# Five zero matmuls in place of seven, the first piece of x copied out of PSUM in halves, both its value projections ahead of the second piece, and a fill of ones moved behind the fifth piece

## The chip, the core and the metric

The kernel runs on one core of a Trainium2 chip. The core has five engines with queues of their own: TensorE (PE; its weight loads are listed apart as PEld), VectorE (DVE), ScalarE (ACT), GpSimd (POOL) and SyncE (SP), which here only issues DMAs. An engine takes its instructions in the order in which they were written and waits on semaphores for the others. The metric is device time in microseconds, the median of the runs of one program. One execution was also profiled.

## The reference

Two branches of one input x (2048 rows of 640 numbers, bf16) are mixed by a gate. The first is a long convolution, done by a Fourier transform. The second is an attention with 32 heads of 20 numbers, in which each row looks at 8 rows, two apart. The start of the kernel works for the second branch.

```python
qkv = (x @ wqkv).reshape(B, S, 3, H, Dh).transpose(2, 0, 3, 1, 4)
q, k, v = qkv[0], qkv[1], qkv[2]
# each row looks at the rows s, s-2, ..., s-14
attn = softmax(mask(einsum("bhsd,bhswd->bhsw", q, kg) * scale))
b = einsum("bhsw,bhswd->bhsd", attn, vg).transpose(0, 2, 1, 3).reshape(B, S, D) @ wo
return g * a + (1 - g) * b
```

## The kernel before

x comes in eight pieces of 256 rows (`xn`, DMAs of 320 KB on SyncE's queue, line 413). For each piece TensorE makes ten transposes of 128 x 128 (line 445): five for its even rows, five for its odd rows, which lie apart because the attention looks two rows back. One copy (line 245 on VectorE, line 243 on ScalarE) brings the result from PSUM to `xT`. The value projection (`vproj`, line 521) takes 121 rows of `xT` and the first half of Wv, five matmuls of 320 columns a unit, and its result goes by a cast into `VW`. The query and key projections (`qkproj`, line 568) take five matmuls of 342 or 349 columns a unit, and their results go by a cast into `stg`, from where DMAs bring each head's rows to `qb` and `kb` (line 618) for the scores.

`VW` holds for each head 20 values and a 21st column of ones, so that the matmul of the attention weights gives the sum of the weights as well. The ones are written by a memset of 576 single elements in each partition, 42 bytes apart (line 431), and for 7 rows of two blocks the column is set to zero (line 433, 32 elements each). Both stand at the start of VectorE's queue, behind a memset of zeros (line 398), which the first matmuls read, and one of `ETall` (line 430).

Seven matmuls of zeros (line 401, `WARM`) keep TensorE busy until the first piece lands. Four more, of 512 columns, follow the transposes of the first piece (line 447); nobody reads what they write. They are called fills here.

What stands where isn't chosen by a scheduler. Each part of the work is a generator that asks for one step after the other, and a string of letters (`ORDER`) says whose step comes next; a dash takes the second of the engines that the step allows (in "AD", VectorE). `a` is the transposes and copies of x, `w` the first half of the value projection, `i` the query and key projection. PSUM is handed out in four slots by the same list. A piece is marked as ready for its readers (`xT0` to `xT7`) when its copy has been written down.

Of the kernel before, what the change touches and what calls it, by code (L numbers as in the profile page):

```python
# [18 lines left out]
D = 640  # L19
L = 4096  # L20
H = 32
DH = 20
NDT = 5
# [5 lines left out]
NBP = 9  # L29
NB = 2 * NBP  # L30
PRE = 7
X0 = 16
HS = 1024
HP = HS + 16
XW = X0 + 2 * HP
# [9 lines left out]
PL = 40  # L45
QC = 160
CR = 8
WARM = 7
KROWS = [(42, 64), (20, 42), (0, 20)]
TAIL = [(0, 3), (3, 3), (6, 2), (8, 3), (11, 3), (14, 2)]  # L50
LAND = dict(W0=9600.0, Wv0=5600.0, W1=23000.0, Wv1=25500.0, x=[4200.0, 7000.0, 8100.0, 10700.0, 11800.0, 12900.0, 14000.0, 15200.0], k=[20300.0])
# [61 lines left out]

STREAMS = "abcdefghijklmnopqrstuvwxyz0123456789ABCDEFGHIJKLMNOPQRSTUVWXYZ"
ORDER = """
a-aa-aw-wa-aw-ww-wiiai-iiaaiaa-aia-iii-aiaa-ii-iiii-ii-iiiicifffccccw-wwww-wwwwfwwwwf-wffffwwwwwwcwcccccwwwdw-wdwddddi-wfccccccii
-iiidfifddiiiieiifiiffiieidddiiiiiicddiwdxwexxxxxxxxxxccccffcfffffffffeccc-xcfcccccccccccccccccccccccccccccccccccccccccccidi-iiddd
ii-iddifd-iifxdddxedidffdfddefcicccii-iddiedd-icddlie-iiiyf-yddccdixiyyfy-xe-ydddexixdxddyyfyy-xcccxcccxffcccccccccccccciiiiciiccd
ciieddffdcccffdd-iiieiifiidididxdiffffffexididxdfeidid-i-xfxxyyy-yyexyey-xyyfyxccccccccciccccc-xcccc-idddidx-i-xxddddi-x-ijdddfjff
# [96 lines left out]
def kernel(  # L216
# [14 lines left out]
    nc = tc.nc  # L231
# [6 lines left out]
    def raw(ap, off, dims):  # L238
        return bass.AP(tensor=ap.tensor, offset=ap.offset + off, ap=dims)

    def copy(eng, dst, src):
        if eng == "A":
            nc.scalar.copy(dst, src)  # L243
        else:
            nc.vector.tensor_copy(dst, src)  # L245
# [7 lines left out]
    def psum(g, k=0, dt=F32):  # L253
        b = g.banks[k]
        v = PS[:, b[0], b[1]] if isinstance(b, tuple) else PS[:, b]
        return v.bitcast(dt) if dt != F32 else v
# [12 lines left out]
    VW = p0.tile([128, NB, H, DH + 1], BF, name="VW", tag="VW")  # L269
# [27 lines left out]
    xT = pL.tile([128, NDT, XW], BF, name="xT")  # L297
# [9 lines left out]
    def ev(name):  # L307
        if name not in E:
            E[name] = Ev()
        return E[name]  # L310

    def mark(name, g, lag=0.0):
        x = ev(name)
        x.src, x.lag = g.done.src, lag

    def at(name, t):
        ev(name).src, ev(name).lag = -1, t
# [73 lines left out]
    def masks(e):  # L391
        nc.gpsimd.memset(ksets[e][:, KW:], 0.0)
        nc.gpsimd.tensor_copy(ksets[e][:, 0:KW].rearrange("p (b k) -> p b k", k=BK), mm[:, 0:BK].unsqueeze(1).to_broadcast([128, NB, BK]))
        nc.gpsimd.tensor_copy(qsets[e][:].rearrange("p (b k) -> p b k", k=BQ), mm[:, BK:BK + BQ].unsqueeze(1).to_broadcast([128, NB, BQ]))

    def heads():
        z = pab[:, 0].rearrange("p n c -> p (n c)")
        nc.vector.memset(z, 0.0)
        wu = PS[:, 0]
        for n in range(WARM):  # L400
            nc.tensor.matmul(wu[:, n % 2, :], lhsT=z[:, 0:128], rhs=z[:, 0:512], start=True, stop=True, skip_group_check=True)
        nc.scalar.dma_start(ident[:], ca["ident"].ap())
        nc.scalar.dma_start(mm[:], ca["mm"].ap())
        at("ET", 4000.0)
        for a in range(8):
            if a == 1:
                nc.sync.dma_start(Wv[:, :, 0:320], W3[:, :, 2, 0:320])
                at("Wv0", LAND["Wv0"])
            if a == 3:
                for w in range(2):  # L410
                    nc.sync.dma_start(Wqk[:, :, w, 0:128], W3[:, :, w, 0:128])
                    at(f"W0{w}", LAND["W0"])
            nc.sync.dma_start(xn[:, a], raw(x2, 256 * a * D, [[2 * D, 128], [D, 2], [1, D]]))
            at(f"x{a}", LAND["x"][a])
        n0, n1 = KROWS[0]
        for q in range(4):
            nc.sync.dma_start(wraw[32 * q:32 * q + 32].rearrange("p c j -> p (c j)"), raw(A_shift_k, 4 * QC * q, [[0, 32], [1, 4 * QC]]))
        for q in range(4):
            nc.sync.dma_start(kin[32 * q:32 * q + 32, 3 + n0:3 + n1, :], raw(k2, n0 * D + QC * q, [[64 * D, 32], [D, n1 - n0], [1, QC]]))
        for q in range(4):  # L420
            at(f"k0{q}", LAND["k"][0])
        for w in range(2):
            nc.sync.dma_start(Wqk[:, :, w, 128:D], W3[:, :, w, 128:D])
            at(f"W1{w}", LAND["W1"])
        nc.sync.dma_start(Wv[:, :, 320:640], W3[:, :, 2, 320:640])
        at("Wv1", LAND["Wv1"])
        nc.gpsimd.memset(xT[:, :, 0:X0], 0.0)
        for c in range(2):
            nc.gpsimd.memset(xT[:, :, X0 + HP * c + HS:X0 + HP * (c + 1)], 0.0)
        nc.vector.memset(ETall[:, :, :, 3 * BQ:], 1.0)  # L430
        nc.vector.memset(VW[:, :, :, DH], 1.0)
        for j in (0, NBP):
            nc.vector.memset(VW[0:PRE, j, :, DH], 0.0)
        for q in range(4):
            nc.gpsimd.memset(kin[32 * q:32 * q + 1, 0:3, :], 0.0)
        for e in range(3):
            masks(e)

    def xpose():
        for a in range(8):  # L440
            g = yield Req("P", 0.0, [ev(f"x{a}")], take=1, pe=(10, 53.0, 110.0, 53.3) if a else (14, 98.8, 200.0, 98.8))
            tx = psum(g, dt=BF)
            for e in range(2):
                for dt in range(NDT):
                    nc.tensor.transpose(tx[:, e, 128 * dt:128 * dt + 128], xn[:, a, e, 128 * dt:128 * dt + 128], ident[:])
            for n in range(0 if a else 4):
                nc.tensor.matmul(PS[:, 3, 0], lhsT=ident[:], rhs=xn[:, 0, n % 2, 0:512], start=True, stop=True, skip_group_check=True)
            r = yield Req("AD", dict(A=1120.0, D=735.0), [g.done], give=g.banks)
            dst = xT[:, 0:1, X0 + 128 * a:X0 + 128 * a + 128]
            dst = raw(dst, 0, [dst.ap[0], [HP, 2], [XW, NDT], [1, 128]])  # L450
            copy(r.eng, dst, tx[:, :, 0:128 * NDT].rearrange("p e (t n) -> p e t n", t=NDT))
            mark(f"xT{a}", r)
        mark("xtr", g)

    def h0_slot():
# [437 lines left out]
    def final():  # L893
# [3 lines left out]
        for n, (t0, m) in enumerate(TAIL):  # L897
# [30 lines left out]
            for gg in range(4):  # L928
                (nc.scalar if n == len(TAIL) - 1 and gg > 1 else nc.sync).dma_start(raw(outf, (32 * (gg // 2) + gg % 2 + 2 * t0) * D, [[64 * D, 32], [2 * D, m], [1, D]]),
                                  reg[32 * gg:32 * gg + 32])  # L930

    heads()
    for gen in (xpose, h0_slot, fragger, score_gen, pv_gen, conv, conv_v, conv_end, qkproj, gate, x_slot, h_slot, p2_slot,
                u_slot, swaps, load_T, load_wo, op_tr, outproj, final):
        plan.add(gen(), gen.__name__)
# [34 lines left out]
```

## Time and profile before

| | |
|---|---|
| median of 3 runs | 224.88 us (224.69 to 225.51) |
| span of the profiled execution, first to last instruction | 222.5 us |
| what the median has above that span | 2.4 us |
| TensorE busy | 204.3 us, 92% of the span |
| VectorE busy | 185.0 us, 83% |
| ScalarE busy | 174.9 us, 79% |
| GpSimd busy | 51.1 us, 23% |

For the profiled execution no time of its own is listed beside its span. A row of the timeline gives start and length in microseconds, the engine, the line, the operation, what it writes and reads, the shape and the count; in brackets stands the idle time of the engine ahead of it, and what ended that. "issue" means that the engine waited for nothing that the profile shows. The chain of work that ended last is followed back from the last instruction to what released each step. DVE, ACT and POOL rows have measured lengths; matmuls are pipelined and their ends are modelled.

### The profile page before, as it was taken

The numbers are of one execution on the slowest core, as the hardware profiler recorded it, in microseconds if no ns is written. First come the engines' busy times: TensorE is split into PE (matmuls) and PEld (weight loads), VectorE is DVE, ScalarE is ACT, GpSimd is POOL, SyncE is SP. The second block draws the span as 40 slices with busy tenths as digits, with TensorE's granted clock in tenths as the row PEclk, the third lists the DMA queues.
The fourth block names the chain that finished last, engine by engine and source line by source line (L and its number), as shares of the span: only waits on it lengthen the run. The fifth ranks groups of instructions, "written<-read, shape, count | busy, mean of one in ns | idle before, by whom it ended". The sixth has DMA issues, their size and how long they took to land.

```text
span 222.5 us, 8401 instructions
## 1 busy us (share of the span) xinstructions
PE 204.3 (92%) x3577; PEld 165.8 (75%) x3577; DVE 185.0 (83%) x261; ACT 174.9 (79%) x253; POOL 51.1 (23%) x129
## 2 busy tenths in 40 slices
PE   7999999999999999699997867999999999979990
PEld 3777987696777577466685756889888899979880
DVE  4745778997998898569898978998999997859992
ACT  0264487769998898599999988998999999478770
POOL 7980711470617044402450000000000000000000
PEclk9999999999999999999999699999999999999999
DMA  6999789599999999803993396678567082003645
GB/s 199 349 237 275 188 180 205 133 168 149 208 182 197 163 151 155 140 4 52 183 171 74 85 214 152 172 174 213 122 142 227 4 184 55 3 3 91 152 106 136
DMA packets 69049, 33.35 MB, mean 150 GB/s; under 512 B 51476, under 2 KB 66708, under 8 KB 69012
## 3 DMA queue, kind: packets, MB, share of 16 engines
q1 hardware_dynamic: 65684, 27.66, 61.3%
q0 software_dynamic: 2880, 4.90, 9.9%
q8 instruction: 28, 0.46, 1.0%
q10 hardware_dynamic: 448, 0.26, 0.4%
q14 instruction: 9, 0.07, 0.1%
HBM read 19.51 MB, written 2.62 MB: 100 GB/s over the span
## 4 chain that ended last, share of the span: by engine, by line
PE 51%; DVE 20%; ACT 10%; DMA 8%; issue 7%; POOL 2%; DVEq 0%; POOLq 0%; ACTq 0%
PE PS L568 14%; PE PS L521 8%; ACT ETall L650 6%; PE PS L835 6%; DMA kb<-stg 6%; DVE UC L245 5%; PE PS L869 4%; PE PS L724 4%; PE PS L674 3%; DVE SX L245 3%; PE PS L642 3%; DVE q L926 2%; DVE yb L245 2%; ACT H L243 2%; DVE q L924 2%
## 5 line engine op out<-in xcount | busy, mean ns | idle before, releaser
L650 ACT ACTIVATE ETall<-PS 121x912 bf16<-121x912 f32 (+1 forms) x80 | 63.8, 864 | 8.1 <-PE PS L642 7.7
L568 PE MATMUL PS<-xT,Wqk 128*128 128x342 bf16 (+1 forms) x300 | 49.7, 310 | 0.6 <-ACT stg L243 0.3
L243 ACT CAST UC<-PS 128x1024 bf16<-128x1024 f32 (+2 forms) x49 | 44.4, 1030 | 4.0 <-DVE UC L245 3.1
L568 PEld LDWEIGHTS <-Wqk 128*128 128x128 bf16 x300 | 27.4, 97 | 14.3 <-issue 0.5
L521 PE MATMUL PS<-WvT,xT 128*121 128x320 bf16 x180 | 27.5, 300 | 0.1
L467 DVE TENSOR_TENSOR KX<-KX 128x1280 bf16<-128x1280 bf16 x32 | 25.3, 820 | 0.3
L618 POOL DMA_DIRECT2D qb<-stg x29 | 14.6, 506 | 45.8 <-ACT stg L243 30.5
L869 PE MATMUL PS<-wo,oT 128*128 128x320 bf16 x160 | 24.4, 302 | 0.1
L521 PEld LDWEIGHTS <-xT 128*121 128x121 bf16 x180 | 23.4, 134 | 1.4
L243 ACT CAST stg<-PS 128x363 bf16<-128x363 f32 (+1 forms) x39 | 17.1, 471 | 7.8 <-PE PS L568 7.5
L869 PEld LDWEIGHTS <-oT 128*128 128x128 bf16 x160 | 21.1, 145 | 1.5 <-issue 0.5
L724 PEld LDWEIGHTS <-G 64*128 64x128 bf16 x512 | 18.2, 93 | 4.9 <-issue 3.7
L618 POOL DMA_DIRECT2D kb<-stg x36 | 18.1, 511 | 15.8 <-ACT stg L243 7.6
L642 PE MATMUL PS<-qb,kb 31*128 31x114 bf16 x576 | 16.0, 212 | 5.1 <-DMA kb<-stg 2.3
L245 DVE CAST stg<-PS 128x342 bf16<-128x342 f32 (+1 forms) x21 | 11.0, 522 | 11.7 <-PE PS L568 9.4
L642 PEld LDWEIGHTS <-kb 31*128 31x128 bf16 x576 | 9.4, 93 | 13.5 <-issue 9.8
L674 PEld LDWEIGHTS <-ETall 121*128 121x128 bf16 x576 | 17.4, 96 | 2.1 <-issue 0.5
L674 PE MATMUL PS<-VW,ETall 121*128 121x63 bf16 (+2 forms) x576 | 18.2, 184 | 0.6 <-DVE SX L245 0.3
L835 PE MATMUL PS<-F,Hw 128*128 128x128 bf16 x160 | 18.1, 219 | 0.0
L874 ACT ACTIVATE bl<-PS,omg 128x320 bf16<-128x320 f32 x31 | 16.1, 566 | 2.4 <-PE PS L869 1.9
L835 PEld LDWEIGHTS <-Hw 128*128 128x128 bf16 x160 | 17.9, 114 | 0.0
L245 DVE CAST UC<-PS 128x1024 bf16<-128x1024 f32 x13 | 15.3, 1219 | 2.6 <-ACT UC L243 1.2
(75 smaller groups left out, 334.1 us busy)
## 6 DMA issues: line engine op xcount, KB each, us to landing
xn<-in_A_q_dram SPq DMA_DIRECT2D x8, 320.0 KB
h_lin<-in_A_ssm_k_dram SPq DMA_DIRECT2D x16, 160.0 KB
vin<-in_A_v_dram SPq DMA_DIRECT2D x8, 320.0 KB
Hw<-H SPq DMA_DIRECT2D x8, 320.0 KB
q<-in_A_q_dram SPq DMA_DIRECT2D x8, 320.0 KB
Hw<-SX SPq DMA_DIRECT2D x8, 320.0 KB
kb<-stg POOLq DMA_DIRECT2D x28, 85.1 KB, 5.5
out_dram<-q SPq DMA_DIRECT2D x16, 120.0 KB
```

Source lines behind the costliest of these rows:

```text
L243: nc.scalar.copy(dst, src)
L245: nc.vector.tensor_copy(dst, src)
L467: eng.tensor_tensor(d, kin[:, n + 3 - j:n + 3 - j + m, :], w.to_broadcast([128, m, QC]), ALU.mult)
L521: nc.tensor.matmul(ps[0:BK, 0:320], lhsT=xT[:, dt, s0:s0 + BK], rhs=Wv[:, dt, 320 * hp:320 * hp + 320], start=(dt == 0), stop=(dt == NDT - 1))
L568: nc.tensor.matmul(ps[:, 0:n], lhsT=Wqk[:, dt, w, 128 * ft:128 * ft + 128], rhs=xT[:, dt, s0:s0 + n], start=(dt == 0), stop=(dt == NDT - 1))
L618: (nc.sync if near else nc.gpsimd).dma_start(dst[r0:r0 + rows, 0:wd], stg[fa - f0:fb - f0, 0:wd])
L642: nc.tensor.matmul(psum(g, h4 // 2)[:, h4 % 2, BQ * bb:BQ * bb + BQ], lhsT=kb[r:r + DH + NF, BK * b:BK * b + 128], rhs=qb[r:r + DH + NF, B ...
L650: nc.scalar.activation(ETall[0:BK, e, :, 0:BQ * nb], psum(g, k)[0:BK, :, 0:BQ * nb], ACT.Exp, scale=SCALE)
L674: nc.tensor.matmul(O[:, (b - b0) // 6, c0:c0 + 21 * nh], lhsT=ETall[0:BK, e, hh, BQ * bb:BQ * bb + 128], rhs=VW[0:BK, b, 4 * t + h4:4 * t ...
L724: nc.tensor.matmul(ps[:, c, 160 * jj:160 * jj + 160], lhsT=G[rows, j0 + jj, 64 - 64 * rr:192 - 64 * rr], rhs=Am[rows, rr].rearrange("p o ( ...
L835: nc.tensor.matmul(d, lhsT=st[(key, P)][:, c, o + il // 4, :, il % 4], rhs=M[:, k, :], start=(k == 0), stop=(k == 1), skip_group_check=True)
L869: nc.tensor.matmul(op, lhsT=oT[:, ft].rearrange("p h m a -> p a (h m)")[:, t, :], rhs=wo[:, ft, 320 * n:320 * n + 320], start=(ft == 0), s ...
```

## The change

It has four edits. Of the zero matmuls five are left, and of the four fills after the first piece one. The first piece's ten transposes are copied from PSUM in two copies, one for the even rows and one for the odd rows; the other pieces are copied as before. The order string is rewritten in its first letters, so that both units of the value projection that read only the first piece stand ahead of the transposes of the second. And the ones and zeros of `VW` are no longer written at the start but by whoever writes down the copy of the fifth piece (`a == 4`).

```diff
-WARM = 7
+WARM = 5
...
-a-aa-aw-wa-aw-ww-wiiai-iiaaiaa-aia-iii-aiaa-ii-iiii
+a-a-aw-ww-wa-aa-aw-wiiai-iiaaiaa-aia-iii-aiaa-ii-iiii
...
         nc.vector.memset(ETall[:, :, :, 3 * BQ:], 1.0)
-        nc.vector.memset(VW[:, :, :, DH], 1.0)
-        for j in (0, NBP):
-            nc.vector.memset(VW[0:PRE, j, :, DH], 0.0)
...
-            for n in range(0 if a else 4):
+            for n in range(0 if a else 1):
                 nc.tensor.matmul(PS[:, 3, 0], lhsT=ident[:], rhs=xn[:, 0, n % 2, 0:512], start=True, stop=True, skip_group_check=True)
-            r = yield Req("AD", dict(A=1120.0, D=735.0), [g.done], give=g.banks)
-            dst = xT[:, 0:1, X0 + 128 * a:X0 + 128 * a + 128]
-            dst = raw(dst, 0, [dst.ap[0], [HP, 2], [XW, NDT], [1, 128]])
-            copy(r.eng, dst, tx[:, :, 0:128 * NDT].rearrange("p e (t n) -> p e t n", t=NDT))
+            for e in ((0, 1), (1, 2)) if a == 0 else ((0, 2),):
+                last = e[1] == 2
+                r = yield Req("AD", dict(A=1120.0, D=735.0) if a else dict(A=580.0, D=450.0), [g.done], give=g.banks if last else [])
+                dst = xT[:, 0:1, X0 + 128 * a + HP * e[0]:X0 + 128 * a + 128 + HP * e[0]]
+                dst = raw(dst, 0, [dst.ap[0], [HP, e[1] - e[0]], [XW, NDT], [1, 128]])
+                copy(r.eng, dst, tx[:, e[0]:e[1], 0:128 * NDT].rearrange("p e (t n) -> p e t n", t=NDT))
             mark(f"xT{a}", r)
+            if a == 4:
+                nc.vector.memset(VW[:, :, :, DH], 1.0)
+                for j in (0, NBP):
+                    nc.vector.memset(VW[0:PRE, j, :, DH], 0.0)
```

Because of the added lines, what was line 445 is line 442 afterwards, 447 is 444, 521 is 524, 568 is 571, and the memsets of 431 and 433 are 453 and 455.

On TensorE before, behind the first piece's transposes, the last of four fills is followed by the second piece, which waits for its DMA (a LDWEIGHTS loads the operand that stays, a MATMUL streams the other; `xn` is x as loaded):

```order
L447 LDWEIGHTS ident
L447 MATMUL PS<-xn,ident 128x512
L445 LDWEIGHTS xn [waits DMAHW4_49]
L445 MATMUL PS<-ident,xn 128x128
L445 LDWEIGHTS xn
```

On TensorE after the change, at the same place, one fill is followed by the first unit of the value projection, which waits for VectorE's copy of the first half and, in its first matmul, for the DMA of Wv:

```order
L442 MATMUL PS<-ident,xn 128x128
L444 LDWEIGHTS ident
L444 MATMUL PS<-xn,ident 128x512
L524 LDWEIGHTS xT [waits DVE_49,Pool_49]
L524 MATMUL PS<-WvT,xT 121x320 [waits DMAHW3_49]
L524 LDWEIGHTS xT
```

A second such unit follows it, and then the second and third piece back to back, where before they had one unit of the value projection between them.

VectorE's queue from its start, as a difference (rows with a minus stood there before, rows with a plus stand there now; `xT<-PS` is a copy of a piece, `VW<-PS` a cast of a value projection, `stg<-PS` a cast of a query or key projection):

```order
 L398 MEMSET KX 128x640
 L430 MEMSET ETall 128x18x128
-L431 MEMSET VW 128x576
-L433 MEMSET VW 7x32 x2
+L245 COPY xT<-PS 128x5x128 x2
+L245 CAST VW<-PS 121x16x20 x2
 L245 COPY xT<-PS 128x2x5x128 x2
 L245 CAST VW<-PS 121x16x20
+L245 CAST stg<-PS 128x342
+L453 MEMSET VW 128x576
+L455 MEMSET VW 7x32 x2
 L245 COPY xT<-PS 128x2x5x128
```

The three memsets of `VW` have moved from the queue's start to a place between the cast of the second query unit and the copy of the sixth piece (number 5, counted from 0), and two casts now stand ahead of the copies of the second and third piece, where one stood between them. ScalarE, GpSimd and SyncE have the same rows in the same order as before.

More of the change, by code (lines that the diff above doesn't have):

```diff
@@ L115 @@
 ORDER = """
-a-aa-aw-wa-aw-ww-wiiai-iiaaiaa-aia-iii-aiaa-ii-iiii-ii-iiiicifffccccw-wwww-wwwwfwwwwf-wffffwwwwwwcwcccccwwwdw-wdwddddi-wfccccccii
+a-a-aw-ww-wa-aa-aw-wiiai-iiaaiaa-aia-iii-aiaa-ii-iiii-ii-iiiicifffccccw-wwww-wwwwfwwwwf-wffffwwwwwwcwcccccwwwdw-wdwddddi-wfccccccii
 -iiidfifddiiiieiifiiffiieidddiiiiiicddiwdxwexxxxxxxxxxccccffcfffffffffeccc-xcfcccccccccccccccccccccccccccccccccccccccccccidi-iiddd
```

## The prediction

> **What bounds the kernel now.** I read the page first, for the span and for who holds the chain that ended last.
>
> ```profile
> span 222.5 us, 8401 instructions
> PE 51%; DVE 20%; ACT 10%; DMA 8%; issue 7%; POOL 2%; DVEq 0%; POOLq 0%; ACTq 0%
> ```
>
> Half of the chain is TensorE. The change touches the first 16 us, so the next view is the chain in order of time (start, length, work).
>
> ```profile
> 1.60 3.17 PE PS L401 x7
> ...
> 15.67 1.46 PE PS L568 x10
> 17.68 4.43 PE PS L568 x30
> 22.12 8.15 PE PS L521 x60
> ```
>
> From the zero matmuls to the 60 value-projection matmuls that end at 30.27, every longer piece of the chain is TensorE. A microsecond lost or won before 22 us has no idle time to vanish in, and I carry it to the end one for one. The early stage in detail is the timeline of TensorE (start, length; ends are modelled, so I measure from start to start).
>
> ```profile
> 1.60 3.17 PE L401 MATMUL PS<-KX 128*128 128x512 bf16 x7 [1.60 <-DVE KX L398]
> 4.57 1.27 PE L445 MATMUL PS<-ident,xn 128*128 128x128 bf16 x10
> 5.63 1.63 PE L447 MATMUL PS<-xn,ident 128*128 128x512 bf16 x4
> 7.12 0.73 PE L445 MATMUL PS<-ident,xn 128*128 128x128 bf16 x10
> 7.71 0.86 PE L521 MATMUL PS<-WvT,xT 128*121 128x320 bf16 x5
> 8.41 0.72 PE L445 MATMUL PS<-ident,xn 128*128 128x128 bf16 x10
> 8.97 1.52 PE L521 MATMUL PS<-WvT,xT 128*121 128x320 bf16 x10
> 10.33 0.89 PE L568 MATMUL PS<-xT,Wqk 128*128 128x342 bf16 x5
> ...
> 13.08 1.28 PE L445 MATMUL PS<-ident,xn 128*128 128x128 bf16 x20
> 14.20 0.91 PE L568 MATMUL PS<-xT,Wqk 128*128 128x349 bf16 x5
> 14.95 0.72 PE L445 MATMUL PS<-ident,xn 128*128 128x128 bf16 x10
> 15.51 1.62 PE L568 MATMUL PS<-xT,Wqk 128*128 128x342 bf16 x10
> ```
>
> Ten transposes take 1.06 us at first (4.57 to 5.63) and 0.56 to 0.59 from 7.12 on: TensorE runs at half speed until about 6.9, where the last fill begins. Seven zero matmuls take 2.97, so 0.424 each. Warm, a value projection of five matmuls takes 0.68 and a unit of the query projection 0.72. Two rows, one of SyncE and one of the weight loads, give the landings that matter.
>
> ```profile
> 5.97 0.89 SPq L413 DMA_DIRECT2D xn<-in_A_q_dram  x1
> 7.12 0.56 PEld L445 LDWEIGHTS <-xn 128*128 128x128 bf16 x10 [0.48 <-DMA xn<-in_A_q_dram]
> ```
>
> The first is the issue of piece 6, which waits for the landing of the first half of Wv (it reuses that load's semaphore): Wv is there at 5.97 at the latest, and the issue before ended at 5.86. The second waits for piece 1 of x (pieces are counted from 0), which lands at 7.1.
>
> **Part one: the front of TensorE (WARM, split copy, both projections early).** Two zero matmuls and three fills go: 2 x 0.424 and 3 x 0.424 at half speed, 2.1 us of TensorE time that computed nothing. That isn't the gain, because piece 1 still lands at 7.1 and both projections still need Wv at 5.97. Step by step: the five zero matmuls end at 3.72; piece 0 is there by 4.57 at the latest, so its ten transposes (1.06) end between 4.8 and 5.6, and the five of its first half by 5.1. A copy of a whole piece takes 0.82 on VectorE (rows below), half of one I put at 0.49 (between 0.41 and 0.82); with VectorE free, the first half is out by about 5.8, the second by 6.3. The first projection starts at 6.0, when Wv is there. At half speed one of its matmuls takes 0.424 x 320/512 = 0.265, so three and a half run until 6.9 and the rest at 0.137: it ends at 7.1. The second follows to 7.8. So one projection of 0.68 has moved ahead of piece 1's landing, not two. Piece 1 then takes 7.8 to 8.36, piece 2 8.36 to 8.92.
>
> Now VectorE is late instead. Its early rows:
>
> ```profile
> 1.98 1.98 DVE L430 MEMSET ETall<- 128x2304 bf16 x1 [0.43 <-issue]
> 5.99 0.54 DVE L431 MEMSET VW<- 128x576 bf16 x1 [2.03 <-issue]
> 6.64 0.93 DVE L245 COPY xT<-PS 128x1280 bf16<-128x1280 bf16 x1
> 6.69 0.23 DVE L433 MEMSET VW<- 7x32 bf16 x2
> 7.89 0.82 DVE L245 COPY xT<-PS 128x1280 bf16<-128x1280 bf16 x1 [0.32 <-PE PS L445]
> 8.63 0.48 DVE L245 CAST VW<-PS 121x320 bf16<-121x320 f32 x1
> ```
>
> Ahead of the copy of piece 1 now stand two casts of 0.48, the later one from about 8.0 to 8.5. The copy (0.82) ends at 9.35, that of piece 2 at 10.2, and the first query unit, which waits for piece 2, starts at 10.2 to 10.25 against 10.33. **Gain of part one: 0.1 us**, of 0.68 at most.
>
> **Part two: the memsets of VW, moved to the middle of the transposes.** They now stand on VectorE behind the cast of the second query unit and ahead of the copy of piece 5.
>
> ```profile
> 12.54 0.52 DVE L245 CAST stg<-PS 128x342 bf16<-128x342 f32 x1 [1.51 <-PE PS L568]
> 14.40 0.82 DVE L245 COPY xT<-PS 128x1280 bf16<-128x1280 bf16 x1 [1.35 <-PE PS L445]
> 15.22 0.54 DVE L245 CAST stg<-PS 128x363 bf16<-128x363 f32 x1
> 15.78 0.82 DVE L245 COPY xT<-PS 128x1280 bf16<-128x1280 bf16 x1
> ```
>
> The hole there is 1.35 us, and by their records the memsets last 0.54 + 0.23 = 0.77. The question is whether the records tell all. Before L431 stands an idle time of 2.03 us that waits for nothing shown: the memset of ETall ended at 3.96, L431 ends at 6.53, the two small ones at 6.92. Counted from end to end, L431 took 6.53 - 3.96 = 2.57 us for 576 elements, 4.46 ns each; each element stands 42 bytes behind the one before. VectorE has one more operation on single elements far apart, L773, with 128 bytes between elements:
>
> ```profile
> L773 DVE TENSOR_TENSOR h_lin<-h_lin,Dz 128x80 bf16<-128x80 bf16 x2 | 1.0, 516 | 0.0
> L467 DVE TENSOR_TENSOR KX<-KX 128x1280 bf16<-128x1280 bf16 x32 | 25.3, 820 | 0.3
> L756 DVE TENSOR_TENSOR Hw<-UC,Hw 128x640 bf16<-128x640 bf16 x2 | 1.0, 486 | 0.0
> ```
>
> From 640 to 1280 elements a tensor-tensor grows from 486 to 820 ns, 0.52 ns an element on a fixed 152. L773 takes 516 for 80: 364 over the fixed part, 4.55 ns an element. Two operations agree within 2%, so I take the unexplained idle time as part of the memset, and the moved block as 6.92 - 3.96 = 2.96 us; its bounds are 0.77 and 2.96.
>
> [...]
>
> The price: the cast ahead ends at 13.06 - 0.1 = 12.96, the block at 15.92, the copy of piece 5 at 16.75. TensorE has finished the transposes of piece 6 by 15.4 and stands before the ten matmuls of L568 that began at 15.51, which read piece 5: they begin at 16.8. Loss against before: **1.3 us**, the 0.1 of part one being used up inside it. Queued behind on VectorE are the cast of 0.54 and the copy of piece 6, which end at 18.1; the matmuls that need them come after the ten (16.8 + 1.44), so they cost nothing more. ScalarE's copy of piece 7 and the 30 matmuls after it follow TensorE and shift with it. The query and key fragments go out by DMA from evictions of those units, so they shift too.
>
> VectorE saves its old wait in front, which hid behind piece 1's landing anyway. SyncE's and GpSimd's queues keep their order.
>
> **Sum.** On the profiled execution: 222.5 + 1.3 = 223.8. The median of the runs, 224.88, lies 2.4 above that span (what stands around the first and last instruction), and the same 2.4 is added: **226.2 us**.
>
> **Rivals.**
>
> 1. The block is short, and the result is not slower. If the 2.03 us belonged to the place and not to the memset, 0.77 us end at 13.7, piece 5 isn't held, and 0.1 us remains: 224.8. It decides as soon as the block takes less than 1.3 us, since piece 5's copy can start at 14.3. What speaks for it is GpSimd:
>
> ```profile
> 4.16 2.00 POOL L393 COPY kb<-mm 128x2178 bf16<-128x2178 bf16 x1 [0.85 <-DMA mm<-ca_mm]
> 6.11 1.89 POOL L394 COPY qb<-mm 128x2052 bf16<-128x2052 bf16 x1
> ```
>
> The first of these copies nearly covers the idle time. Against it: it starts 0.2 us after VectorE was free, and L431 ran on from 6.11 to 6.53 beside the second. If such copies did block, another one would run at the new place too. [...]
>
> 2. The clock stays low. Fewer zero matmuls and fills leave TensorE two holes of together 0.5 to 0.8 us between 3.4 and 6.85. Stretches of one length, with TensorE's busy time and the granted clock after the engines:
>
> ```profile
> 92.17:95.59 3.42, 2.08 (x37) 1.33 (x38) 0.51 (x1) 1.70 (x3) 0.00 (x0) 1.00 0.34 101
> 119.48:122.89 3.41, 1.98 (x48) 1.28 (x48) 2.64 (x4) 3.41 (x6) 0.00 (x0) 1.00 0.41 88
> 122.89:126.30 3.41, 3.26 (x54) 2.75 (x55) 3.27 (x4) 3.41 (x4) 0.19 (x1) 0.50 0.42 109
> ```
>
> 1.98 us of 3.41 lost the clock for one such stretch, 2.08 kept it, and 3.26 brought it back. The change leaves 2.6 or more, which should do, but no row shows what is enough to raise it. If it isn't, half speed lasts one stretch longer, to 10.26: two projections (1.33 each) end at 8.7, pieces 1 and 2 at 10.3, the query unit starts at 11.7, 1.5 later than in my sum, and the block behind it shifts along: 227.7. [...]
>
> 3. The front gains in full: VectorE keeps up, piece 1 goes 0.68 us earlier, and the block is short: 224.2.
>
> **How the numbers follow.** Forecast 0.58, rival one 0.25, rival two 0.11, rival three 0.06. The forecast's own range is 225.5 to 226.9 (a later wait may swallow or add half a microsecond). The range 224.5 to 227.1 takes in rival one and leaves out rivals two and three. About 0.5% (1.1 us) is what a measurement here can tell from no change: faster means under 223.8, slower over 226.0. Slower: rival two and 0.39 of the forecast's 0.58, 0.50. Faster: the edge of rival three, 0.04. Same: the rest, 0.46.
>
> **What would show it.** In the changed profile, the first of the ten L568 matmuls that now start at 15.51 should start near 16.8, waiting for VectorE; the VW memset should again show an idle time near 2 us that waits for nothing, ending about 15.5; the query unit should start at 10.2. If the memset sits right behind its cast and piece 5's copy starts by 14.4, part two is wrong and rival one holds. If the transposes of piece 1 take 1.06, the clock is rival two. If the start is 1.3 late at 22 us and the end is not, the carrying one for one was wrong.

## The result, and the profile after

The changed kernel takes 226.36 us (median of 20 runs, 223.92 to 228.55), the kernel before beside it 224.74 (20 runs, 222.52 to 227.54). The ratio is 1.007, with a 95% interval of 1.0042 to 1.0099: slower by 0.9 to 2.2 us. The forecast was 226.2. Here and below medians are over all runs, while a ratio leaves out the runs more than 1.5% above the fastest of their kernel (of twelve runs 6 stay for the second measurement of the ones on GpSimd, 11 for the change beside it), so the two can differ by up to 0.8%.

The profiled execution of the changed kernel took 225.35 us, with a span of 223.6 against 222.5. The page's span and its chain by engine:

```profile
span 223.6 us, 8393 instructions
PE 38%; DVE 21%; DMA 19%; ACT 9%; issue 7%; POOL 2%; SPq 1%; DVEq 0%; POOLq 0%; ACTq 0%
```

TensorE has fallen from 51% to 38% of the chain. That alone says little about the cause: up to 31.5 us the chain is now followed back through transfers, where before it went through TensorE's rows. Two of its longer pieces:

```profile
7.51 7.17 DMA xn<-in_A_q_dram
...
25.84 5.66 DMA kb<-stg
```

Neither tells why the start is later. The timeline of TensorE in the changed kernel is the better view (start, length, line; in brackets the idle time and its releaser):

```profile
6.25 1.52 PE L524 MATMUL PS<-WvT,xT 128*121 128x320 bf16 x10 [1.21 <-DMA WvT<-in_B_wqkv_dram]
7.61 1.56 PE L442 MATMUL PS<-ident,xn 128*128 128x128 bf16 x20
...
10.09 0.89 PE L571 MATMUL PS<-xT,Wqk 128*128 128x342 bf16 x5
...
14.70 0.72 PE L442 MATMUL PS<-ident,xn 128*128 128x128 bf16 x10
16.48 1.63 PE L571 MATMUL PS<-xT,Wqk 128*128 128x342 bf16 x10 [1.06 <-DVE xT L245]
...
22.94 8.31 PE L524 MATMUL PS<-WvT,xT 128*121 128x320 bf16 x60
```

The first query unit starts 0.24 us earlier than before (10.09 against 10.33). The ten matmuls that read piece 5 start 0.97 later (16.48 against 15.51), and TensorE idled 1.06 ahead of them, waiting for VectorE's copy. The 60 matmuls of the value projection then start at 22.94. In the same view of the kernel before they stand at

```profile
21.95 8.31 PE L521 MATMUL PS<-WvT,xT 128*121 128x320 bf16 x60
```

so 0.99 of the delay is still there 6 us on, and 1.1 at the end of the span. VectorE in the changed kernel:

```profile
4.49 0.89 DVE L245 COPY xT<-PS 128x640 bf16<-128x640 bf16 x2 [0.54 <-PE PS L442]
...
12.29 0.51 DVE L245 CAST stg<-PS 128x342 bf16<-128x342 f32 x1 [1.63 <-PE PS L571]
14.84 0.54 DVE L453 MEMSET VW<- 128x576 bf16 x1 [2.03 <-issue]
15.49 0.93 DVE L245 COPY xT<-PS 128x1280 bf16<-128x1280 bf16 x1
15.55 0.23 DVE L455 MEMSET VW<- 7x32 bf16 x2
```

The memset is recorded with 0.54 us again, and again 2.03 us ahead of it wait for nothing shown. The cast ahead of it ended at 12.80 and it ended at 15.38, so the pair of gap and record lasts 2.57 or 2.58 at the start of the queue and in its middle. TensorE's row at 14.70 is already piece 6's transposes, so what the copy of piece 5 reads was there.

### The profile page after: what moved, and what is told of

It is laid out like the page before. It is cut to its first block, busy times and chain, and to the rows that moved or that the text cites. A ratio compares the mean times of both kernels' runs of the same rounds, so it can differ in the third digit from the quotient of the medians.

```text
span 223.6 us, 8393 instructions
## 1 busy us (share of the span) xinstructions
PE 202.8 (91%) x3572; PEld 165.0 (74%) x3572; DVE 185.2 (83%) x262; ACT 175.1 (78%) x253; POOL 51.0 (23%) x129
## 4 chain that ended last, share of the span: by engine, by line
PE 38%; DVE 21%; DMA 19%; ACT 9%; issue 7%; POOL 2%; SPq 1%; DVEq 0%; POOLq 0%; ACTq 0%
PE PS L571 10%; DMA kb<-stg 8%; DMA xn<-in_A_q_dram 6%; PE PS L838 6%; ACT ETall L653 5%; DVE UC L245 5%; PE PS L727 4%; DVE SX L245 4%; PE PS L872 4%; PE PS L524 4%; PE PS L677 3%; PE PS L645 3%; DMA Wqk<-in_B_wqkv_dram 3%; DVE q L929 2%; DVE yb L245 2%
## 5 line engine op out<-in xcount | busy, mean ns | idle before, releaser
L245 DVE CAST UC<-PS 128x1024 bf16<-128x1024 f32 x13 | 15.3, 1219 | 2.6 <-ACT UC L243 1.2
```

## The experiments

The theory under test: the strided memset itself holds VectorE for 2.6 us, wherever it stands, and this delays the ten matmuls. Rival one (the "place theory"): the idle time belonged to the place at the start, and the memset is short. Rival two: the front loses TensorE's clock. Rival three: the front gains more than 0.1 us.

One measure serves for all kernels: the time from the start of the first query unit to the start of the ten matmuls that read piece 5. It is 5.17 or 5.18 us with every front that was run, as long as no whole block stands in between.

| kernel | first projection, ten matmuls | first query unit | ten matmuls on piece 5 | between | median us (before beside it) |
|---|---|---|---|---|---|
| before | old order | 10.33 | 15.51 | 5.18 | 224.74 |
| change | 1.52 | 10.09 | 16.48 | 6.39 | 226.36 (224.74) |
| change, again | 1.52 | 9.52 | 15.91 | 6.39 | 225.44 (224.94) |
| block moved alone | old order | 10.37 | 16.77 | 6.40 | 226.66 (225.34) |
| flat memset at the place | 1.52 | 9.41 | 14.59 | 5.18 | 224.70 (225.34) |
| block split in two | 2.45 | 10.61 | 15.78 | 5.17 | 225.45 (225.34) |
| ones on ScalarE | 2.37 | 10.19 | 15.37 | 5.18 | 224.86 (225.34) |
| ones on GpSimd | 1.52 | 9.79 | 14.96 | 5.17 | 225.72 (225.34) |
| ones on GpSimd, again | 1.52 | 10.00 | 15.17 | 5.17 | 224.83 (224.94) |
| the same with seven zero matmuls | 1.54 | 9.41 | 14.59 | 5.18 | 224.64 (224.94) |
| before, ones on GpSimd | old order | 10.82 | 15.99 | 5.17 | 224.85 (224.94) |
| front alone | 2.90 | 12.82 | 17.99 | 5.17 | 226.38 (225.34) |
| front alone, again | 2.89 | 12.95 | 18.12 | 5.17 | 227.70 (225.58) |
| six steps (one run) | 2.90 | 15.38 | 21.76 | 6.38 | 230.74 |

**The block moved alone.** The kernel before, with only the fourth edit:

```diff
-        nc.vector.memset(VW[:, :, :, DH], 1.0)
-        for j in (0, NBP):
-            nc.vector.memset(VW[0:PRE, j, :, DH], 0.0)
...
             mark(f"xT{a}", r)
+            if a == 4:
+                nc.vector.memset(VW[:, :, :, DH], 1.0)
+                for j in (0, NBP):
+                    nc.vector.memset(VW[0:PRE, j, :, DH], 0.0)
```

> The kernel before with one edit: the three memsets of VW stand behind the copy of piece 4. Block theory (the memsets hold VectorE for 2.96 us wherever they stand): the cast ahead ends at 13.06, the copy of piece 5 about 2.9 + 0.82 later, the ten L568 matmuls start near 16.7 in place of 15.51, the span grows by 1.2 us, ratio 1.005 to 1.006. Front theory (the loss comes from fewer zero matmuls, the split copy or the order of the projections): no change, ratio 1.000. Place theory (the 2.03 us of idle time belonged to the start of the queue): the block takes 0.8 us, fits the hole, ratio 1.000.

Measured: 226.66 against 225.34, ratio 1.0063 (1.0023 to 1.0103). VectorE, then TensorE, in this kernel's timelines:

```profile
12.58 0.51 DVE L245 CAST stg<-PS 128x342 bf16<-128x342 f32 x1 [1.52 <-PE PS L569]
15.13 0.54 DVE L451 MEMSET VW<- 128x576 bf16 x1 [2.03 <-issue]
15.78 0.93 DVE L245 COPY xT<-PS 128x1280 bf16<-128x1280 bf16 x1
```

```profile
10.37 0.89 PE L569 MATMUL PS<-xT,Wqk 128*128 128x342 bf16 x5
...
16.77 1.63 PE L569 MATMUL PS<-xT,Wqk 128*128 128x342 bf16 x10 [1.06 <-DVE xT L245]
```

The same rows as in the changed kernel, idle times of 2.03 and 1.06 included. The moved block alone gives the whole loss: 1.26 at the ten matmuls (16.77 against 15.51), more than the 0.97 of the four edits together.

**The same place with a memset of neighbours.** Again 576 elements on VectorE at that place, but in nine runs of 64 that lie side by side (it writes ones where ones stand already). The ones and zeros of `VW` go to GpSimd.

```diff
         for e in range(3):
             masks(e)
+        nc.gpsimd.memset(VW[:, :, :, DH], 1.0)
+        for j in (0, NBP):
+            nc.gpsimd.memset(VW[0:PRE, j, :, DH], 0.0)
...
             if a == 4:
-                nc.vector.memset(VW[:, :, :, DH], 1.0)
-                for j in (0, NBP):
-                    nc.vector.memset(VW[0:PRE, j, :, DH], 0.0)
+                nc.vector.memset(ETall[:, :, 0, 3 * BQ:3 * BQ + 64], 1.0)
```

> The changed kernel with the ones of VW on GpSimd, and at the old place behind piece 4 a VectorE memset of as many elements (576), but in nine runs of 64 that lie side by side (it rewrites ones of ETall). Block theory (cost per element that lies far from the last): the memset takes about 0.6 us from the cast before it to its end, no 2 us idle time, the ten matmuls start near 15.25, ratio 0.999. Place theory (GpSimd's mask copy beside it, or the place itself, holds a memset back): the idle time of 2.03 us stands ahead of it again and the ten matmuls start at 16.4.

Measured: 224.70 against 225.34, ratio 0.9963 (0.9922 to 1.0004). VectorE:

```profile
11.62 0.51 DVE L245 CAST stg<-PS 128x342 bf16<-128x342 f32 x1 [1.51 <-PE PS L572]
12.20 0.54 DVE L456 MEMSET ETall<- 128x576 bf16 x1
13.48 0.83 DVE L245 COPY xT<-PS 128x1280 bf16<-128x1280 bf16 x1 [0.74 <-PE PS L445]
```

The same count at the same place has the same record of 0.54, but it begins 0.07 behind the cast, and the copy of piece 5 waits for TensorE as it did before the change. So the place costs nothing. The strided block, with the same count, has the same record of 0.54 too. For neighbours the record is nearly the whole time: from the end of the cast to that of the memset it is 12.74 - 12.13 = 0.61 us. For the strided block the record is short by 2 us (2.57 from end to end).

**The block split.** Nine of the 18 blocks are written at the start, nine behind piece 4.

```diff
+        nc.vector.memset(VW[:, 0:NBP, :, DH], 1.0)
+        nc.vector.memset(VW[0:PRE, 0, :, DH], 0.0)
...
             if a == 4:
-                nc.vector.memset(VW[:, :, :, DH], 1.0)
-                for j in (0, NBP):
-                    nc.vector.memset(VW[0:PRE, j, :, DH], 0.0)
+                nc.vector.memset(VW[:, NBP:NB, :, DH], 1.0)
+                nc.vector.memset(VW[0:PRE, NBP, :, DH], 0.0)
```

> The changed kernel with the memsets of 9 blocks (288 elements, 1.28 us by the block theory) at the start of VectorE's queue and those of the other 9 behind piece 4. Block theory: the first part ends at about 5.4 and hides behind the landing of Wv at 6.0 to 6.2, the second takes 1.45 us in a hole of 1.35 to 1.5 us, the copy of piece 5 ends before TensorE wants it, the ten L568 matmuls start at 15.3; 0.2 us under before, ratio 0.999. Front theory: still slower by about 1 us, 1.005. Place theory: a full 2 us of idle time stands ahead of the second part too, and half the loss or more stays.

Measured: 225.45 against 225.34, ratio 0.9995 (0.9948 to 1.0043). VectorE, rows of the two halves and of the copy of piece 5:

```profile
4.94 0.30 DVE L431 MEMSET VW<- 128x288 bf16 x1 [0.99 <-issue]
...
14.32 0.30 DVE L455 MEMSET VW<- 128x288 bf16 x1 [0.99 <-issue]
14.70 0.83 DVE L245 COPY xT<-PS 128x1280 bf16<-128x1280 bf16 x1
```

Half the elements have half the gap: 0.99 + 0.30 = 1.29 us. That fits a hole of 1.35 us, and the ten matmuls are held no longer (5.17). They start at 15.78 all the same, where 15.3 was expected, because the first projection's ten matmuls took 2.45 here and the query unit started at 10.61.

**The ones on another engine.** ScalarE writes them at the start (an exponential of zeros, and two copies of zeros), or GpSimd behind its mask copies, with the same three lines that the flat memset's kernel has.

```diff
+        nc.scalar.activation(VW[:, :, :, DH], z[:, 0:NB * H].rearrange("p (b h) -> p b h", h=H), ACT.Exp)
+        for j in (0, NBP):
+            nc.scalar.copy(VW[0:PRE, j, :, DH], z[0:PRE, 0:H])
```

> The changed kernel with no memset of VW on VectorE: ScalarE, idle until 8.4, writes the ones as the exponential of the zeros at its start (and the zeros by two copies). Block theory: the hole on VectorE stays empty, the ten L568 matmuls start near 15.25, 0.25 us under before, span 222.2 to 222.4, ratio 0.999. Front theory: still about 1 us slower than before, 1.005.

> The changed kernel with the three memsets of VW on GpSimd, behind its mask copies (15.65 us; its next work is due at 22.7). Block theory: VectorE's hole stays empty, the ten L571 matmuls start near 15.25, span 222.2 to 222.4, ratio 0.999; if GpSimd too pays some 4.5 ns an element it is done by 18.5 and delays nothing. Front theory: about 1 us slower than before, 1.005.

> The changed kernel with the ones on GpSimd once more, for a narrower interval beside its neighbours in this call: 0.2 us under before by the front part of the prediction, ratio 0.998 to 0.999; the first series gave 0.9956 with an interval that reaches 1.001.

Measured: ScalarE 224.86 against 225.34, ratio 1.0013 (0.996 to 1.0066). GpSimd 225.72 against 225.34, ratio 0.9956 (0.9902 to 1.001); again, 224.83 against 224.94, ratio 0.9916 (0.9869 to 0.9962). The rows of the two fills, ScalarE's and GpSimd's, each from its kernel's timeline:

```profile
2.90 2.76 ACT L431 ACTIVATE VW<-KX 128x576 bf16<-128x576 bf16 x1
```

```profile
15.62 2.65 POOL L435 MEMSET VW<- 128x576 bf16 x1
```

These engines need 2.76 and 2.65 us for the 576 elements, 4.8 and 4.6 ns each, and their records show it whole. On both, the fill is out of the way of the ten matmuls (5.17 and 5.18). In the profiles GpSimd's version is ahead of the change by 0.74 us at the ten matmuls (15.17 against 15.91, measured beside one another), and by 0.6 us in the medians (224.83 against 225.44). The ratios, 0.9916 and 1.0049, lie further apart, but I don't build on them, for the reason given with the result; over all runs the two overlap widely, so that the whole kernel gains is likely and not shown. ScalarE's interval overlaps the change's. Beside the block moved alone (226.66) the split block (225.45) and ScalarE's ones (224.86) have medians 1.2 and 1.8 us lower. Against the kernel before, the two measurements of GpSimd's don't settle it: the medians differ by +0.38 and -0.11 us, the ratios by -0.4% and -0.8%.

**The price by step.** The changed kernel with six more memsets of 288 elements at the start, with 2, 4, 8, 16, 32 and 64 bytes from one element to the next. They are extra work, and what they write is overwritten later.

```diff
+        flat = VW[:].rearrange("p b h e -> p (b h e)")
+        for s in (1, 2, 4, 8, 16, 32):
+            nc.vector.memset(flat[:, 0:288 * s].rearrange("p (n s) -> p n s", s=s)[:, :, 0], 0.0)
```

> A measuring kernel: six more memsets of 288 elements each on VectorE behind that of ETall, into VW, with steps of 2, 4, 8, 16, 32 and 64 bytes. Block theory: from end to end about 0.3 us each while elements share a short line, and 288 x 4.46 = 1.28 us each from some step on, at the latest at 32 bytes. Place theory: the idle time doesn't follow the step. The kernel as a whole is later by 3 to 5 us at the front.

VectorE's rows, in the order of the steps:

```profile
3.96 0.30 DVE L433 MEMSET VW<- 128x288 bf16 x1
4.41 0.30 DVE L433 MEMSET VW<- 128x288 bf16 x1 [0.15 <-DVE VW L433]
5.18 0.30 DVE L433 MEMSET VW<- 128x288 bf16 x1 [0.47 <-DVE VW L433]
6.59 0.30 DVE L433 MEMSET VW<- 128x288 bf16 x1 [1.11 <-issue]
7.94 0.30 DVE L433 MEMSET VW<- 128x288 bf16 x1 [1.05 <-issue]
9.32 0.30 DVE L433 MEMSET VW<- 128x288 bf16 x1
```

Every record is 0.30 long, whatever the step. Their ends show what they really take: 4.26, 4.71, 5.48, 6.89, 8.24, 9.62. From end to end they take 0.30, 0.45, 0.77, 1.41, 1.35 and 1.38 us, so 1.0, 1.6, 2.7, 4.9, 4.7 and 4.8 ns an element (from the second on with the short wait for the memset ahead, which writes the same columns). The cost grows with the step up to 16 bytes and is flat from there; 42 bytes, with 4.5 ns an element in the block, lies on the flat part. The expectation had 0.3 us up to some step and 1.28 beyond it; the rows of 4 and 8 bytes, 0.45 and 0.77 us, stand in between. An estimate from these rows, 0.5 ns an element and another 0.26 ns for each byte of the step up to 16, gives 1.0, 1.5, 2.6 and, from 16 bytes on, 4.7.

The same kernel settles what spoke for rival one in the prediction, GpSimd's copies beside the memset. Its block in the middle comes so late that GpSimd has ended its last copy (at 15.54) and does nothing until 29.49, and the gap is the same:

```profile
17.58 0.51 DVE L245 CAST stg<-PS 128x342 bf16<-128x342 f32 x1 [1.51 <-PE PS L574]
20.12 0.54 DVE L456 MEMSET VW<- 128x576 bf16 x1 [2.03 <-issue]
```

```profile
13.65 1.89 POOL L394 COPY qb<-mm 128x2052 bf16<-128x2052 bf16 x1
29.49 0.66 POOL L624 DMA_DIRECT2D kb<-stg  x1 [13.95 <-DVE KX L473]
```

**The front alone.** The changed kernel with the block put back to the start.

```diff
         nc.vector.memset(ETall[:, :, :, 3 * BQ:], 1.0)
+        nc.vector.memset(VW[:, :, :, DH], 1.0)
+        for j in (0, NBP):
+            nc.vector.memset(VW[0:PRE, j, :, DH], 0.0)
...
             mark(f"xT{a}", r)
-            if a == 4:
-                nc.vector.memset(VW[:, :, :, DH], 1.0)
-                for j in (0, NBP):
-                    nc.vector.memset(VW[0:PRE, j, :, DH], 0.0)
```

> The changed kernel with the three memsets back at the start of VectorE's queue. Block theory: they end at 6.9 as before, the first half of piece 0 is copied by 7.4, the first projection starts at 7.4 in place of 6.25, the first query unit near 11.2 against 10.33 before, span 0.7 to 0.9 us above that of before, ratio about 1.004. Front theory: slower than before by the whole 1.1 us of the changed kernel. Place theory: the same as the block theory, since the place is the old one.

> The kernel with the new front and the VW block back at the start, run once more. If the late start of the first query unit (12.82 us, where 11.2 was expected) is what this order does, because VectorE is held until 6.9 us and TensorE stands idle so long that its clock rises one stretch later, the unit starts at 12.5 to 13.0 again and the median stands 0.5 to 2 us above the kernel before. If it was the chance of that one profiled run, the unit starts near 11.2 and the median within 0.7 us of the kernel before. In both cases the ten matmuls that read piece 5 start 5.17 us behind it.

Measured: 226.38 against 225.34, ratio 1.0045 (1.0005 to 1.0086); again, 227.70 against 225.58, ratio 1.0107 (1.0045 to 1.017). The first expectation had the query unit at 11.2; it started at 12.82 and, the second time, at 12.95. VectorE and TensorE in the second:

```profile
5.98 0.54 DVE L431 MEMSET VW<- 128x576 bf16 x1 [2.02 <-issue]
6.63 0.59 DVE L245 COPY xT<-PS 128x640 bf16<-128x640 bf16 x1
...
7.16 0.46 DVE L245 COPY xT<-PS 128x640 bf16<-128x640 bf16 x1
```

```profile
4.97 0.63 PE L447 MATMUL PS<-xn,ident 128*128 128x512 bf16 x1
7.37 2.89 PE L523 MATMUL PS<-WvT,xT 128*121 128x320 bf16 x10 [1.77 <-DVE xT L245]
10.06 1.80 PE L445 MATMUL PS<-ident,xn 128*128 128x128 bf16 x20
...
12.95 0.89 PE L570 MATMUL PS<-xT,Wqk 128*128 128x342 bf16 x5
...
18.12 1.62 PE L570 MATMUL PS<-xT,Wqk 128*128 128x342 bf16 x10
```

The early block holds the half copies until 6.6, TensorE stands idle for 1.77 us behind its one fill, and the ten matmuls of the first piece's value projection then take 2.89 where they take 1.52 in the changed kernel: half speed. This is rival two's loss, and it stands in all three profiles that have the new front and a whole block, or the six steps, at the start (2.89, 2.90 and 2.90). Two profiles without that, the split block's and ScalarE's, have part of it (2.45 and 2.37) behind idle times of only 0.32 and 0.20, so that the idle time alone brings it is not shown. The half speed is read from the matmuls' lengths only, since the table of windows has a granted clock of 1.00 (the third number from the end) for that stretch:

```profile
6.83:10.24 3.41, 2.87 (x12) 2.43 (x13) 1.28 (x4) 0.00 (x0) 3.41 (x4) 1.00 1.12 338
```

**Controls of the front.** The kernel before with its ones on GpSimd (the three lines moved as above), so an empty VectorE with the old front; and seven zero matmuls in place of five, in the kernel with the ones on GpSimd.

```diff
-WARM = 5
+WARM = 7
```

> The kernel before with one edit: the three memsets of VW on GpSimd behind its mask copies. Block theory: in the kernel before the block was hidden behind the landing of piece 1, so taking it off VectorE gains nothing: first query unit at 10.3 to 10.5, ratio 1.000. If the block had held up the start there too: 0.5 us under before, 0.998.

> The changed kernel with the ones on GpSimd and seven zero matmuls again. If the start is bound by the landing of Wv (front part of the prediction): the first projection still starts when Wv lands, 6.0 to 6.2, and nothing changes against five, ratio 0.998 to 0.999. If fewer zero matmuls cost clock (rival two): this one is ahead of the kernel with five by some tenths of a microsecond.

> The changed kernel itself, on the same chip as its variants: 1.0 to 1.5 us above before, ratio 1.005 to 1.007, and as much above the variant with the ones on GpSimd.

Measured: the kernel before with its ones on GpSimd, 224.85 against 224.94, ratio 0.9979 (0.9939 to 1.0018); seven zero matmuls, 224.64 against 224.94, ratio 1.0023 (0.9982 to 1.0063); the change again, 225.44 against 224.94, ratio 1.0049 (0.9992 to 1.0105), so 0.5 us in the medians where 1.0 to 1.5 was expected. TensorE in the first of them:

```profile
7.65 0.73 PE L445 MATMUL PS<-ident,xn 128*128 128x128 bf16 x10 [0.81 <-DMA xn<-in_A_q_dram]
...
10.82 0.89 PE L568 MATMUL PS<-xT,Wqk 128*128 128x342 bf16 x5
```

With the old order of TensorE, an early free VectorE gained nothing in front: TensorE waited 0.81 us for piece 1 to land, and the first query unit started at 10.82 against 10.33. Five zero matmuls or seven isn't settled: the median with seven is 0.2 us lower than with five beside it (224.64 against 224.83), the ratio higher (1.0023 against 0.9916).

## Why the prediction was right, step by step

**The moved block: right.** The prediction took the unexplained 2.03 us as part of the memset, on the strength of one other row with far-apart elements. The block alone, the flat memset at the same place, the half block and the six steps all bear it out, and rival one falls. The gross price is the same in all four profiles that have the whole block there: 6.38 to 6.40 against 5.17 or 5.18 without, so 1.2 us. The prediction's own working comes to 1.3 at the start of the ten matmuls with a gain of 0.1 in front, so 1.4 gross, 0.2 too much: from the end of the cast to the end of piece 5's copy it had 2.96 + 0.82 = 3.78, measured are 16.42 - 12.80 = 3.62, since the records of the copy and of the two small memsets lie beside one another. Net, the term "Loss against before: 1.3 us" measured 0.97: the block cost 0.18 less than it had, and the front gained 0.14 more.

**Carried to the end one for one: right in the profiled pair, not shown beyond it.** 0.97 at the ten matmuls, 0.99 at 22.94, 1.1 in the span. Other single profiles don't agree so well. The change's second one is 0.40 later than before at the ten matmuls and 1.2 at the end, and the flat memset's kernel is 0.92 earlier there and its span 1.7 longer (224.2 against 222.5). Over all profiles, what comes in behind the ten matmuls runs from -0.9 to +2.6 us beside the kernel before, more than the half microsecond that the prediction allowed. The medians of the change give 1.6, with 0.9 to 2.2 in the interval, those of the block moved alone 1.3 for 1.26 at the ten matmuls, and those of the front alone 1.0 and 2.1 for 2.48 and 2.61.

**The front: right in kind, mis-sized.** The term "Gain of part one: 0.1 us" measured 0.24 in the profiled pair, and the prediction's second projection, which it had end at 7.8, ended at 7.61. Two assumptions of that step move from run to run. Wv landed later than the 5.97 it took (the projection waited 1.21 for it, until 6.25). And the clock, which it kept low until 6.9, was already up by then: the ten matmuls took 1.52 to 1.54 in six of the eight profiles that have the new front and no whole block at the start, and 2.37 and 2.45 in the two others. In these eight the first query unit starts from 9.41 to 10.61, mean 9.88; with the old front it starts at 10.33, 10.37 and 10.82, mean 10.51. The front is worth some 0.6 us by these means, more than predicted, though not as an amount that every run gets, and the runs of the whole kernel don't resolve it. That is near rival three's 0.68, but its way isn't what happened: piece 1's transposes don't start 0.68 earlier (7.04 to 8.24 in the eight, against 7.12 before), and VectorE doesn't keep up, since in six of the eight TensorE waits 0.32 to 0.36 us for its copy of piece 1.

**Rival two's figures.** It counted on 2.6 us or more of busy TensorE from 3.4 to 6.85. In the profiled change it was 2.21, because of the wait for Wv, and in the front alone 2.02 and 2.18. That the clock came up in the change was therefore not worked out but lucky: there it was up before that wait, since the one fill took 0.38 (at 4.66) where it takes 0.63 at half speed. By its own 1.06 for ten transposes its pieces 1 and 2 would also end at 10.5 and not at 10.3, which the forecast doesn't use. Half speed "to 10.26" is its estimate from the one half-clock stretch of 3.41 us in its rows. In the two profiles of the front alone the ten matmuls from 7.37 to 10.06 were slow (2.90 and 2.89), and the 20 transposes from 10.06 on took 1.67 and 1.80 where five of the eight profiles above have 1.28; where in them the clock rose isn't shown.

**"VectorE saves its old wait in front, which hid behind piece 1's landing anyway": right for the old front, wrong as a statement about the new one.** With the old front the saving is worth nothing (10.37 and 10.82 against 10.33). With the new one it is worth 2.2 us at the least (12.82 against 10.61) and 3.5 at the most (12.95 against 9.41), because the half copies run from 4.49 when VectorE is free, and only from 6.63 when it isn't, and TensorE's clock stays low meanwhile (2.89 and 2.90 for the ten matmuls, against 1.52 to 2.45). The sum came out right since it worked out the front with the block already gone. For the front alone that sentence makes it wrong, a gain of 0.1 where 2.5 and 2.6 were lost (17.99 and 18.12 against 15.51). Alone, the move costs 1.26 at the ten matmuls, so the two parts added are 3.7 to 3.9, and together they cost 0.97.

**The time around the span: an offset that happened to fit.** The prediction added 2.4, a median less another execution's span. The profiled execution has 225.35 - 223.6 = 1.75, and every run on record has 1.7 to 2.0. So some 0.6 of the 2.4 was that the profiled execution of the kernel before was faster than its median one. The median of the changed kernel lies 1.0 above its profiled execution, more again. Forecast and result for the span were 223.8 and 223.6; that the time came within 0.2 us as well (226.2 against 226.36) is in part luck.

What stays open: how much the change gains over the kernel before once the ones are on another engine. The profiles put the ten matmuls at 14.59 to 15.37 against 15.51, 0.1 to 0.9 us earlier; the medians and the ratios don't agree on whether it reaches the end. Why the clock rises at different times in kernels with the same start (the one fill took 0.38 at 4.66 in the change's first profile and 0.63 at 4.95 in its second) wasn't tried either.

## What to carry to other kernels

An idle time just ahead of an instruction that waits for nothing shown may be that instruction itself (here 2.03 of 2.57 us): count from end to end, and compare with another operation on elements as far apart. The fills of single elements 16 to 64 bytes apart took 4.5 to 4.9 ns an element here, whatever the step: such a fill is best priced by its count and put on an engine whose queue has a hole of that length. Two edits that look separate can each lose and still lose less together (here 1.26 and 2.48 or 2.61 us alone, 0.97 together), so work out each part with the other in place.

## What the runs showed of the hardware that wasn't expected

- The record of a VectorE memset followed its count alone: 0.30 us for 288 elements at steps of 2 to 64 bytes and 0.54 for 576 side by side or 42 bytes apart, while the real length of 288 ran from 0.30 to 1.41. ScalarE's and GpSimd's records of theirs were whole (2.76 and 2.65 us).
- Three engines paid nearly the same for an element 42 bytes behind the one before: 4.5 ns on VectorE (2.57 us for 576), 4.8 on ScalarE, 4.6 on GpSimd.
- A VectorE memset cost more the further its elements lay apart, up to a step of 16 bytes: at 2, 4, 8 and 16 bytes from one element to the next 1.0, 1.6, 2.7 and 4.9 ns an element, and no more at 32 and 64 (4.7 and 4.8).
- In front, TensorE still ran at half speed after an idle time of 1.77 us (2.89 for ten matmuls, from 7.37 on), while a granted clock of 1.00 was listed.
